# Loading each K and V tile of a decode attention kernel through two DMA queues instead of one

## The chip, the core and the metric

The kernel runs on one core of a Trainium2 chip. The metric is the device time of one execution in microseconds, given as the median over several runs. A core has five engines with instruction streams of their own: PE (matmul), DVE (vector), ACT (scalar activation), POOL (GpSimd) and SP (SyncE, which here only issues transfers). Transfers from the chip's main memory (HBM) to the on-chip buffer are made by 16 DMA engines; SP, ACT and POOL can each put transfers into a queue of its own.

## What is computed

One decode step of attention (8 sequences, 32 heads, 4096 keys, head size 128) and an MLP beside it, on the same normalized input; both are added to x.

```python
xn = _layernorm(x)
q = (xn @ wq).reshape(B, Sq, Hq, Dh).transpose(0, 2, 1, 3)        # B=8, Sq=1, Hq=32, Dh=128
scores = jnp.einsum("bhqd,bhkd->bhqk", q, k_cache) * (Dh ** -0.5)  # Sk=4096 keys
o = jnp.einsum("bhqk,bhkd->bhqd", _softmax(scores), v_cache)
return x + o.reshape(B, Sq, Hq * Dh) @ wo + mlp(layernorm(xn))     # MLP 640 -> 1728 -> 640
```

All inputs are bf16. The two caches are 268 MB each and every byte of them is used once, so nearly everything that is read is cache.

## The kernel before

**Items.** The work is cut into NQ = 32 items: item i is one sequence and a group of HS = 8 heads. The 8 heads of 4096 keys lie over the 128 partitions, 16 partitions for each head and NKEY = 256 keys in each partition. A K tile or a V tile is thus 128 partitions of 256 keys x 128 numbers, 64 KB in a partition and 8.39 MB in all.

**Buffers.** `S_sb` has three slots of one tile each: K of the even items (KA), K of the odd items (KB), and V (VS). K(i) can be loaded when item i-2 is done with its slot, V(i) when item i-1 is done with the only V slot.

**The steps of an item.** `k_ready` is a small POOL memset (`kr_sb`) behind a wait for K(i); PE waits for it. `dve_chunk` (three of them) computes q.k for 176 of the 256 keys on DVE: a multiply by the broadcast query (`qbc_sb`), an add of halves, a reduction into `Sd_sb`. The other 80 keys are transposed on PE (`pe_T`), evicted by ACT (`act_T`) and multiplied on PE (`pe_QK`); `dve_sel` picks their scores. `dve_max` finds the maximum, `act_exp` makes the eight rows of `P_sb`; its end is the ticket `exp`. `pe_PV` multiplies with V in 256 matmuls; its end is the ticket `pv`. `o_norm` on POOL scales the result into `oT_sb`, and `qrep` on POOL prepares the query of the next item once the last `pe_QK` of the present one is done.

**What sets the order.** The order is a table of numbers: `at(pos, fn, i)` records a call, all calls are sorted by `pos`, and each engine gets its instructions in that order. An item is Q = 100 positions long and o = 100 i. K(i) is at o-51, V(i) at o+50, `k_ready` at o-2, `qrep` at o-52, `o_norm` at o+175. SP carries all cache and weight loads in this order; ACT's queue has a few small ones and POOL's none. In SP's stream V(i-1) follows K(i).

**The waits of the loads.** `load_k` waits for `exp` of item i-2 (from item KLATE = 6 on; before that for the last transposes `kt` and the last reduction `km` of item i-2). `load_v` waits for `pv` of item i-1. The next-to-last V tile, V(30), is loaded in two pieces cut at key 192 (`V_CUT`), so that PV can begin on the first. After K(31), V(30), the MLP weights (`load_mlp`, `load_w2b`) and V(31), the last loads are those of wo (`load_wl`, `load_wn`), which take K's second slot when item 31 has let it go. At the end stand PV of item 31, `pe_sel` and `dve_fold`, the last products with wo (`fin_wl`, `fin_wn`) and the store.

Here are the functions that the change touches:

Of the kernel before, what the change touches and what calls it, by code (L numbers as in the profile page):

```python
# [192 lines left out]
def bass_parallel_sum__gqa_block_cached__mixer_channel_mlp__decode_kernel(  # L193
# [19 lines left out]
    NKEY = SK * HS // P  # L213
    NHQ = H // HS
    NQ = NHQ * B
# [15 lines left out]
    KLATE = 6  # L231
    assert NKEY == 256 and NQ == 32
    SLOT = NKEY * DH
    KA, KB, VS = 0, 1, 2
# [2 lines left out]
    NL = 3  # L237
    WN_CUT = (0, 5 * CT, 7 * CT, 7 * CT + CT // 2, HS * CT)
    V_CUT = (0, 192, 256)

    def jp_of(i):
        return 80
# [6 lines left out]
    def kslot(i):  # L249
        return KA if i % 2 == 0 else KB  # L250
# [8 lines left out]
    with ExitStack() as es:  # L259
        sb = lambda name, shape, dt: es.enter_context(nc.sbuf_tensor(name, shape, dt))  # L260
        ps = lambda name, shape, dt: es.enter_context(nc.psum_tensor(name, shape, dt))
        sem = lambda name: es.enter_context(nc.semaphore(name))

        S_sb = sb("S_sb", [P, 3, SLOT], BF)
        tile = [S_sb[:, s, :].rearrange("p (j d) -> p j d", d=DH) for s in range(3)]
# [6 lines left out]
        def scratch(n, rows=P, slot=KB):  # L272
# [71 lines left out]
        pe, dve, act, sp, pool = (_Eng(sem(f"{n}_s")) for n in ("pe", "dve", "act", "sp", "pool"))  # L344
        pe2, act2, fin, fin2 = (_Eng(sem(n)) for n in ("pe2_s", "act2_s", "fin_s", "fin2_s"))
        ld_s = [_Dma(sem(f"ld_s{s}")) for s in range(3)]
        ld_x, ld_b1, ld_b2, ld_wq, ld_w1, ld_w2a, ld_w2b, st_a, st_o = (
            _Dma(sem(n)) for n in ("ld_x", "ld_b1", "ld_b2", "ld_wq", "ld_w1", "ld_w2a", "ld_w2b", "st_a", "st_o"))
        ld_vl = [_Dma(sem(f"ld_vl{q}")) for q in range(1, len(V_CUT) - 1)]
        ld_wl = [_Dma(sem(f"ld_wl{q}")) for q in range(2)]  # L350
        ld_wn = [_Dma(sem(f"ld_wn{q}")) for q in range(len(WN_CUT) - 1)]
        tk = {}
        prog = []

        def at(pos, fn, *a):
            prog.append((pos, len(prog), fn, a))
# [4 lines left out]
        def cache_src(cache, i):  # L361
            hq, b = divmod(i, B)
            return cache[b, hq * HS:(hq + 1) * HS].rearrange("h (p j) d -> (h p) j d", j=NKEY)

        def load_k(i):
            s = kslot(i)
            if i >= KLATE:
                sp.wait(tk[("exp", i - 2)])
            elif i >= 2:
                sp.wait(tk[("kt", i - 2)], tk[("km", i - 2)])  # L370
            elif s == KB:
                sp.wait(tk["qmm"])
            tk[("k", i)] = ld_s[s].sig(sp.dma_start(tile[s], cache_src(A_k_cache, i)))

        def load_mlp():
            sp.wait(tk[("kt", NQ - 2)], tk[("km", NQ - 2)])
# [1 line left out]
            load("w2a", ld_w2a, w2_sb, B_w2[0:FB * P, :].rearrange("(p c) n -> p c n", c=FB))  # L378

        def load_v(i):  # L380
            sp.wait(tk["qmm"] if i == 0 else tk[("pv", i - 1)])
            if i != NQ - 2:
                tk[("v", i)] = [ld_s[VS].sig(sp.dma_start(tile[VS], cache_src(A_v_cache, i)))]
                return
            tk[("v", i)] = []
            for d, lo, hi in zip([ld_s[VS]] + ld_vl, V_CUT[:-1], V_CUT[1:]):
                if lo:
                    d.n += 1
                tk[("v", i)].append(
                    d.sig(sp.dma_start(tile[VS][:, lo:hi, :], cache_src(A_v_cache, i)[:, lo:hi, :])))  # L390

        def load_b1():
            act.wait(tk[("kt", NQ - 2)], tk[("km", NQ - 2)])
# [295 lines left out]
        def pe_PV(i):  # L689
            PVB.use(pe)  # L690
            pe.wait(tk[("exp", i)])
            for j in range(NKEY):
                if j == 0:
                    pe.wait(tk[("v", i)][0])
                elif j in V_CUT:
                    pe.wait_ge(ld_vl[V_CUT.index(j) - 1].sem, 1)
                last = pe.matmul(PV_ps[:, 0:HS], tile[VS][:, j, :], P_sb[:, :, j],
                                 start=(j == 0), stop=(j == NKEY - 1))
            tk[("pv", i)] = PVB.used(pe, pe2.sig(last))
# [112 lines left out]
        at(NQ * Q - 55, load_mlp)  # L812
        at(NQ * Q - 54.9, load_w2b)
        at(-870, load_k, 0)
        at(NQ * Q - 60.1, zero_w2b)
        at(-800, consts_pool)
# [17 lines left out]
        for i in range(NQ):  # L834
            o = i * Q
            last = i == NQ - 1
            if i:
                at(o - 51, load_k, i)
            at(o + 50, load_v, i)
            at(o - 52, qrep, i)  # L840
            at(o - 2, k_ready, i)
            at(o - 11, pe_qbc, i)
            at(o - 10.5, act_qbc, i)
            nt = jp_of(i) // TPB
            w = 42.0 / nt
            for t in range(nt):
                at(o + w * t, pe_T, i, t)
                at(o + w * (t + 0.4), act_T, i, t)
                at(o + w * (t + 1.5), pe_QK, i, t)
            at(o + 2, dve_chunk, i, 0)  # L850
            at(o + 26, dve_chunk, i, 1)
            at(o + 52, dve_sel, i, 0)
            at(o + 55, dve_sel, i, 1)
            at(o + 58, dve_chunk, i, 2)
            at(o + 84, dve_max, i)
            at(o + 90 if i else o + Q + 45, act_exp, i)
            at(o + Q + 48, pe_RS, i)
            at(o + Q + 57, dve_rinv, i)
            at(o + Q + 50, pe_PV, i)
            if not last:  # L860
                at(o + Q + 71, act_O, i)
            at(o + Q + 75, o_norm, i)
# [3 lines left out]
        o = NQ * Q  # L866
# [21 lines left out]
        head, mid, end, cut, done = [], [], [], [], []  # L888
# [55 lines left out]
```

## Time and profile before

| | |
|---|---|
| median of 3 runs | 1281.35 us (1281.34 to 1282.29) |
| profiled execution, first to last instruction (span) | 1280.1 us |
| what lies around the span (median less span) | 1.25 us |
| the profiled execution's own time, span and surroundings | about 1281.35 us |
| bytes moved | 551.99 MB, 431 GB/s over the span |
| busy: DVE, PE, ACT, POOL | 1101.6, 672.0, 477.0, 109.3 us |
| DMA packets | 10785 |

The trace gives each instruction's start and duration, what ended the idle time before it, and for the DMA queues the packets, bytes and the time that the packets took. SPq in a row is an instruction by which SP issues a transfer. A row "A<-B" in the waits says that A's engine sat idle until B was done. All kernel instructions pass through helpers, so their line is L111 or L109; rows are told apart by their tiles.

### The profile page before, as it was taken

What the parts mean: (1) busy time and instruction counts of PE and PEld (TensorE: products, weight loads), DVE (VectorE), ACT (ScalarE), POOL (GpSimd) and SP (SyncE); (2) the same over time, 40 slices, a digit from 0 to 9 for tenths busy, and PEclk for the clock granted to TensorE, in tenths of its full rate; (3) what the DMA queues carried; (4) which work ended last, traced back from release to release, by engine and by line L of the source; (5) the groups of instructions that cost most, each with busy time, mean ns of one, the idle gap of its engine ahead of it and who ended that gap; (6) DMA issues with size and microseconds to landing.
All of it is one profiled execution on the core that took longest, in us unless ns stands there. A gap on an engine that the chain in (4) does not pass through costs nothing.

```text
span 1280.1 us, 34355 instructions
## 1 busy us (share of the span) xinstructions
PE 672.0 (52%) x13906; PEld 573.2 (45%) x13906; DVE 1101.6 (86%) x681; ACT 477.0 (37%) x906; POOL 109.3 (9%) x119
## 2 busy tenths in 40 slices
PE   1636555446645446545456554456454466464476
PEld 1435444335535345444345444345343355353465
DVE  1899999889888889888898888898888898888894
ACT  0524444233444233443234443234442334442331
POOL 0020010000000000000000000000000000000050
PEclk9755565565565556555555555556555656655665
DMA  9999999999999999999999999999999999999998
GB/s 419 427 433 431 432 430 432 442 432 430 430 442 428 432 432 436 436 430 432 432 442 430 430 432 438 432 430 434 436 436 430 432 430 442 432 428 434 432 440 367
DMA packets 10785, 551.99 MB, mean 431 GB/s; under 512 B 1242, under 2 KB 1523, under 8 KB 1812
## 3 DMA queue, kind: packets, MB, share of 16 engines
q1 hardware_dynamic: 10736, 551.79, 99.7%
q8 instruction: 9, 0.15, 0.0%
q10 hardware_dynamic: 36, 0.02, 0.0%
q14 instruction: 4, 0.03, 0.0%
HBM read 551.80 MB, written 0.01 MB: 431 GB/s over the span
## 4 chain that ended last, share of the span: by engine, by line
DMA 47%; DVE 37%; issue 11%; ACT 4%; DVEq 0%; SPq 0%; PE 0%
DMA S_sb<-in_A_k_cache_dram 45%; DVE S_sb L111 26%; DVE Sd_sb L111 8%; ACT P_sb L111 4%; DMA S_sb<-in_A_wo_dram 2%; DVE S_ps L111 1%; DVE mx_sb L111 1%; DVE mbT_sb L111 0%; DVE mxT_sb L111 0%; DVE ri_sb L111 0%; DVE NB_sb L111 0%; DVEq L109 0%; DVE mq_sb L111 0%; DVE mb_sb L111 0%; SPq L111 0%
## 5 line engine op out<-in xcount | busy, mean ns | idle before, releaser
L111 PE MATMUL TR_ps<-ident_bf,S_sb 128*128 128x128 bf16 (+1 forms) x2570 | 343.3, 280 | 353.5 <-POOL kr_sb L111 333.2
L111 DVE TENSOR_TENSOR S_sb<-S_sb,qbc_sb 128x7552 bf16<-128x7552 bf16 (+1 forms) x96 | 388.7, 4049 | 128.3 <-DMA S_sb<-in_A_k_cache_dram 128.0
L111 PEld LDWEIGHTS TR_ps<-ident_bf,S_sb 128*128 (+2 forms) x2570 | 245.7, 103 | 411.7 <-issue 338.5
L111 DVE TENSOR_REDUCE Sd_sb<-S_sb 128x59 f32<-128x3776 bf16 (+1 forms) x96 | 390.2, 4065 | 6.0
L111 ACT ACTIVATE KT_sb<-TR_ps 128x1024 bf16<-128x1024 bf16 x320 | 327.0, 1024 | 121.6 <-PE TR_ps L111 109.6
L111 PE MATMUL PV_ps<-P_sb,S_sb 128*128 128x8 bf16 x8192 | 224.0, 175 | 140.6 <-DMA S_sb<-in_A_v_cache_dram 137.9
L111 PEld LDWEIGHTS PV_ps<-P_sb,S_sb 128*128 128x128 bf16 x8192 | 221.3, 103 | 143.3 <-DMA S_sb<-in_A_v_cache_dram 140.5
L111 DVE TENSOR_TENSOR S_sb<-S_sb 128x3776 bf16<-128x3776 bf16 (+1 forms) x96 | 206.5, 2151 | 3.3
L111 ACT ACTIVATE P_sb<-Sd_sb,NB_sb 128x256 bf16<-128x256 f32 x256 | 126.3, 494 | 210.9 <-DVE NB_sb L111 210.9
L111 PE MATMUL S_ps<-qrep_sb,KT_sb 128*128 128x8 bf16 x2560 | 121.9, 177 | 50.9 <-ACT KT_sb L111 47.8
L111 ACT ACTIVATE oU_sb<-PV_ps 128x8 f32<-128x8 f32 x31 | 5.5, 178 | 375.8 <-PE PV_ps L111 375.8
L111 PEld LDWEIGHTS S_ps<-qrep_sb,KT_sb 128*128 128x128 bf16 x2560 | 91.7, 103 | 82.4 <-ACT KT_sb L111 41.1
L111 POOL TENSOR_TENSOR oT_sb<-oU_sb,ri_sb 128x8 bf16<-128x8 f32 x31 | 71.8, 2315 | 370.8 <-DVE S_sb L111 315.3
L111 POOL COPY qrep_sb<-qT_sb 128x128 bf16<-128x128 bf16 x32 | 18.3, 573 | 474.7 <-PE S_ps L111 455.1
L111 ACT ACTIVATION_READ_ACCUMULATOR P_sb<-Sd_sb,NB_sb 128x1 f32 x256 | 47.8, 187 | 0.0
L111 DVE TENSOR_TENSOR S_ps<-S_ps,mask_sb 128x320 f32<-128x320 f32 (+1 forms) x65 | 31.6, 486 | 2.7 <-PE S_ps L111 2.7
L111 DVE TENSOR_REDUCE Sd_sb<-S_ps 128x40 f32<-128x320 f32 x64 | 31.5, 492 | 2.2
L111 PE MATMUL QB_ps<-ident_bf,qrep_sb 128*128 128x128 bf16 x32 | 9.1, 285 | 40.7 <-DVE S_sb L111 22.1
L111 ACT ACTIVATE qbc_sb<-QB_ps 128x128 bf16<-128x128 f32 x32 | 8.9, 278 | 57.6 <-PE QB_ps L111 57.6
L111 POOL MEMSET kr_sb<- 128x1 f32 x32 | 3.2, 99 | 294.9 <-DMA S_sb<-in_A_k_cache_dram 294.9
L111 PEld LDWEIGHTS QB_ps<-ident_bf,qrep_sb 128*128 128x128 bf16 x32 | 3.3, 103 | 43.6 <-ACT oU_sb L111 29.0
L111 PE MATMUL CH_ps<-rs_sb,ones_f 128*128 128x8 f32 x64 | 15.4, 313 | 6.5 <-ACT P_sb L111 6.5
(68 smaller groups left out, 150.6 us busy)
## 6 DMA issues: line engine op xcount, KB each, us to landing
S_sb<-in_A_v_cache_dram SPq DMA_DIRECT2D x1, 6144.0 KB, 26.8
S_sb<-in_A_wq_dram SPq DMA_DIRECT2D x1, 5120.0 KB, 15.6
S_sb<-in_A_wo_dram SPq DMA_DIRECT2D x1, 2560.0 KB, 18.4
S_sb<-in_B_w_dram SPq DMA_DIRECT2D x1, 2160.0 KB, 30.3
S_sb<-in_B_w_dram SPq DMA_DIRECT2D x1, 2080.0 KB, 34.9
S_sb<-in_A_v_cache_dram SPq DMA_DIRECT2D x1, 2048.0 KB, 31.4
S_sb<-in_A_wo_dram SPq DMA_DIRECT2D x1, 1280.0 KB, 21.1
S_sb<-in_A_wo_dram SPq DMA_DIRECT2D x1, 800.0 KB, 22.6
```

What stands on the lines that cost most here:

```text
L111: inst = getattr(e, name)(*a, **k)
```

## The change

From item 2 on, each K load, and from item 0 on each V load, is written as two loads of 128 keys each: the first half goes into SP's queue as before, the second into POOL's, which thereby issues DMAs for the first time. Each half has its own semaphore (`ld_s` for SP, `ld_g` for POOL) and both have the waits that the whole load had. V(30) becomes three: keys 0 to 96 on SP, 96 to 192 on POOL, 192 to 256 on SP. Who waited for a load now waits for both halves. `load_k` moves from o-51 to o-101 from item 2 on, which places it behind `k_ready` of item i-1 and ahead of `qrep` of item i. K(0), K(1), and all weights are loaded by SP as before.

```diff
+    KH = NKEY // 2
...
+        ld_g = [_Dma(sem(f"ld_g{s}")) for s in range(3)]
...
         def load_k(i):
             s = kslot(i)
-            if i >= KLATE:
-                sp.wait(tk[("exp", i - 2)])
-            elif i >= 2:
-                sp.wait(tk[("kt", i - 2)], tk[("km", i - 2)])
-            elif s == KB:
-                sp.wait(tk["qmm"])
-            tk[("k", i)] = ld_s[s].sig(sp.dma_start(tile[s], cache_src(A_k_cache, i)))
+            if i < 2:
+                if s == KB:
+                    sp.wait(tk["qmm"])
+                tk[("k", i)] = ld_s[s].sig(sp.dma_start(tile[s], cache_src(A_k_cache, i)))
+                return
+            tk[("k", i)] = []
+            for e, d, lo in ((sp, ld_s[s], 0), (pool, ld_g[s], KH)):
+                if i >= KLATE:
+                    e.wait(tk[("exp", i - 2)])
+                else:
+                    e.wait(tk[("kt", i - 2)], tk[("km", i - 2)])
+                tk[("k", i)].append(d.sig(e.dma_start(
+                    tile[s][:, lo:lo + KH, :], cache_src(A_k_cache, i)[:, lo:lo + KH, :])))
...
         def load_v(i):
...
+            end = V_CUT[1] if i == NQ - 2 else NKEY
+            parts = [(sp, ld_s[VS], 0, end // 2), (pool, ld_g[VS], end // 2, end)]
+            if end < NKEY:
+                ld_vl[0].n += 1
+                parts.append((sp, ld_vl[0], end, NKEY))
             tk[("v", i)] = []
+            for e, d, lo, hi in parts:
+                e.wait(tk["qmm"] if i == 0 else tk[("pv", i - 1)])
                 tk[("v", i)].append(
-                    d.sig(sp.dma_start(tile[VS][:, lo:hi, :], cache_src(A_v_cache, i)[:, lo:hi, :])))
+                    d.sig(e.dma_start(tile[VS][:, lo:hi, :], cache_src(A_v_cache, i)[:, lo:hi, :])))
...
-                    pe.wait(tk[("v", i)][0])
+                    pe.wait(tk[("v", i)][:2])
...
-                at(o - 51, load_k, i)
+                at(o - 51 if i < 2 else o - 101, load_k, i)
```

In POOL's stream of the first items, this is what stands there before (`kr_sb` is `k_ready`, `qrep_sb` is `qrep`, `oT_sb` is `o_norm`; rows from `qrep` of item 0 to `o_norm` of item 0, with what each waits for):

```order
L111 COPY qrep_sb<-qT_sb 128x128 [waits dve_s]
L111 MEMSET kr_sb 128x1 [waits ld_s0]
L111 COPY qrep_sb<-qT_sb 128x128 [waits pe_s]
L111 MEMSET oT_sb 128x8
L111 MEMSET kr_sb 128x1 [waits ld_s1]
L111 COPY qrep_sb<-qT_sb 128x128 [waits pe_s]
L111 TENSOR_TENSOR oT_sb<-oU_sb,ri_sb 128x8 [waits dve_s,act_s]
```

And now, from the same `qrep` of item 0 on:

```order
L111 COPY qrep_sb<-qT_sb 128x128 [waits dve_s]
L111 MEMSET kr_sb 128x1 [waits ld_s0]
L111 COPY qrep_sb<-qT_sb 128x128 [waits pe_s]
L111 DMA S_sb<-in_A_v_cache_dram 128x16384
L111 MEMSET oT_sb 128x8
L111 MEMSET kr_sb 128x1 [waits ld_s1]
L111 DMA S_sb<-in_A_k_cache_dram 128x16384 [waits dve_s]
L111 COPY qrep_sb<-qT_sb 128x128 [waits pe_s]
L111 DMA S_sb<-in_A_v_cache_dram 128x16384 [waits pe2_s]
L111 TENSOR_TENSOR oT_sb<-oU_sb,ri_sb 128x8 [waits dve_s,act_s]
```

Behind each `k_ready` there is now the second half of the next K, and between `qrep` and `o_norm` the second half of a V. The first DMA, that of V(0), stands behind `k_ready` of item 0 and `qrep` of item 1, which SP's half does not.

At the end of SP's stream, from K(31) on (a number in a row is the elements in a partition: 16384 is half a tile):

```order
L111 DMA S_sb<-in_A_k_cache_dram 128x16384 [waits act2_s]
L111 DMA S_sb<-in_A_v_cache_dram 128x12288 [waits pe2_s]
L111 DMA S_sb<-in_A_v_cache_dram 128x8192
L111 DMA S_sb<-in_B_w_dram 128x8640 [waits dve_s,pe_s]
L111 DMA S_sb<-in_B_w_dram 128x8320
L111 DMA S_sb<-in_B_w_dram 4x1280 [waits pool_s]
L111 DMA S_sb<-in_B_w_dram 4x1280 x7
L111 DMA S_sb<-in_A_v_cache_dram 128x16384 [waits pe2_s]
```

Before, the rows of K(31) and V(31) had 32768 elements and the first of V(30) had 24576; their places and all rows of the weights (`in_B_w`, `in_A_wo`) are the same. In POOL's stream the second half of V(31) now comes behind the two copies of `sel_pool`:

```order
L111 MEMSET kr_sb 128x1 [waits ld_g1,ld_s1]
L111 MEMSET S_sb 48x1280 [waits dve_s]
L111 COPY S_sb<-ident_bf 128x2048
L111 COPY S_sb<-ident_bf 128x1024
L111 DMA S_sb<-in_A_v_cache_dram 128x16384 [waits pe2_s]
L111 TENSOR_TENSOR oT_sb<-oU_sb,ri_sb 128x8 [waits dve_s,act_s]
```

The DMA row is the only new one; the rest stood in this order before.

More of the change, by code (lines that the diff above doesn't have):

```diff
@@ L380, in load_v @@
         def load_v(i):
[L381 to L384, printed above, removed]
+            end = V_CUT[1] if i == NQ - 2 else NKEY
[3 more added lines that the diff above has]
+                parts.append((sp, ld_vl[0], end, NKEY))
             tk[("v", i)] = []
-            for d, lo, hi in zip([ld_s[VS]] + ld_vl, V_CUT[:-1], V_CUT[1:]):
-                if lo:
-                    d.n += 1
+            for e, d, lo, hi in parts:
+                e.wait(tk["qmm"] if i == 0 else tk[("pv", i - 1)])
                 tk[("v", i)].append(
-                    d.sig(sp.dma_start(tile[VS][:, lo:hi, :], cache_src(A_v_cache, i)[:, lo:hi, :])))
+                    d.sig(e.dma_start(tile[VS][:, lo:hi, :], cache_src(A_v_cache, i)[:, lo:hi, :])))
         def load_b1():
```

## The prediction

> **What bounds the kernel now.** I read the page's slices first, then its DMA queues, then one item of the middle in the timeline.
>
> ```profile
> span 1280.1 us, 34355 instructions
> DMA  9999999999999999999999999999999999999998
> GB/s 419 427 433 431 432 430 432 442 432 430 430 442 428 432 432 436 436 430 432 432 442 430 430 432 438 432 430 434 436 436 430 432 430 442 432 428 434 432 440 367
> q1 hardware_dynamic: 10736, 551.79, 99.7%
> ```
>
> The DMA engines are busy 99.7% of the span with the packets of one queue, SP's, at a flat 430 to 442 GB/s; only the first two slices and the last are lower. So the kernel is bound by how fast the 16 engines move 552 MB. DVE, 86% busy, is second. The next question is how far ahead the loads are issued, since that says what a later issue would cost.
>
> ```profile
> 558.70 0.33 SPq L111 DMA_DIRECT2D S_sb<-in_A_k_cache_dram  x1
> 558.87 4.03 DVE L111 TENSOR_TENSOR S_sb<-S_sb,qbc_sb 128x7424 bf16<-128x7424 bf16 x1 [4.27 <-DMA S_sb<-in_A_k_cache_dram]
> 578.15 7.00 PE L111 MATMUL PV_ps<-P_sb,S_sb 128*128 128x8 bf16 x256 [4.86 <-DMA S_sb<-in_A_v_cache_dram]
> 585.18 0.33 SPq L111 DMA_DIRECT2D S_sb<-in_A_v_cache_dram  x1
> 597.41 0.33 SPq L111 DMA_DIRECT2D S_sb<-in_A_k_cache_dram  x1
> 597.56 4.03 DVE L111 TENSOR_TENSOR S_sb<-S_sb,qbc_sb 128x7424 bf16<-128x7424 bf16 x1 [4.25 <-DMA S_sb<-in_A_k_cache_dram]
> S_sb<-in_A_k_cache_dram SPq DMA_DIRECT2D x32, 38.7
> S_sb<-in_A_v_cache_dram SPq DMA_DIRECT2D x31, 31.6
> ```
>
> An item takes 597.41 - 558.70 = 38.7 us, two loads of 19.35 us. K is issued 38.7 us before it lands: 19.35 us of other loads are still queued ahead of it. V is issued 31.6 us ahead, so 31.6 - 19.35 = 12.3 us are queued. These are the margins: a K half may be issued up to 19 us later, a V half up to 12 us, before the DMA engines run dry. DVE waits 4.27 us per item for K and PE 4.86 us for V; both wait because of the rate, and a load that lands later for a while only uses margin.
>
> **What the change does to the rate.** Bytes stay. What changes is the packets: a half has 128 packets of 32 KB where the whole had 128 of 64 KB, and one more set of 16 semaphore packets. What a packet costs beside its bytes can be read by setting a stretch of 64 KB packets against one of small ones. First the DMA view of 600 to 1200 us, then 1265.7 to 1277 us, when wo is loaded:
>
> ```profile
> DMA packets 4464, 260.05 MB, mean 433 GB/s; under 512 B 496, under 2 KB 496, under 8 KB 496
> q1 hardware_dynamic: 4464, 260.05, 100.1%
> ```
>
> ```profile
> DMA packets 718, 4.55 MB, mean 402 GB/s; under 512 B 76, under 2 KB 237, under 8 KB 493
> q1 hardware_dynamic: 718, 4.55, 96.6%
> ```
>
> Time of packets over all 16 engines: 600 x 16 x 1.001 = 9609.6 us and 11.3 x 16 x 0.966 = 174.7 us. With a us per MB and b us per packet: 260.05a + 4464b = 9609.6 and 4.55a + 718b = 174.7. This gives b = 0.0103 us: 10 ns for each packet.
>
> Added packets per engine: 62 tiles (30 K, 32 V; V(30) goes from two pieces to three, also one more) x (128 / 16 data + 1 semaphore) = 558. Times 10.3 ns: 5.7 us. The first stretch's 100.1% says that neighbouring packets overlap by 0.1%, 1.3 us of the run over 10736 / 16 = 671 packets, 2 ns each; that leaves 8.3 x 558 = 4.6 us. I take **+5 us**.
>
> The trace never has two busy queues side by side, so this term needs both bounds. Below: if the engines serve one queue while the other pays its 10 ns, the added packets cost nothing and those of today vanish too, 671 x 10.3 ns = 6.9 us gained. Above: if going from one queue to the other costs as much again as a packet, 62 x 16 = 992 data packets per engine add 10.2 us, so 5.7 + 10.2 = +15.9. I stay near the single-queue rows: there too the next packet already stands in the queue and 8 ns are paid all the same.
>
> **Issue, waits and order.** SP issues a half in 0.33 us as it did a whole; its order is unchanged. POOL's halves are new. K(i+1)'s stands behind `k_ready` of item i, so it waits for K(i) to land besides `exp`; at 558.70 and 558.79 these coincide:
>
> ```profile
> 558.79 0.10 POOL L111 MEMSET kr_sb<- 128x1 f32 x1 [9.88 <-DMA S_sb<-in_A_k_cache_dram]
> 572.93 0.39 POOL L111 COPY qrep_sb<-qT_sb 128x128 bf16<-128x128 bf16 x1 [14.03 <-PE S_ps L111]
> 585.44 2.19 POOL L111 TENSOR_TENSOR oT_sb<-oU_sb,ri_sb 128x8 bf16<-128x8 f32 x1 [12.12 <-DVE S_sb L111]
> ```
>
> Cost 0, covered by 19 us. V(i)'s half waits for `pv`, which ends just before 585.18; `qrep`, ahead of it, is done by 573.3: cost 0, covered by 12 us. Behind POOL's two waits stand `qrep` (14.03 us after the K half's place) and `o_norm` (idle 12.12 us before): free too. How long POOL is busy issuing one DMA no row shows; the bounds are SP's 0.33 us and its longest compute instructions here, some 5 us each (quoted below). Either fits into 12 us. DVE and PE each wait for one semaphore more, tens of nanoseconds inside 4.27 and 4.86 us of waiting: 0.
>
> At the start POOL's half of V(0) comes behind `qrep` of item 1:
>
> ```profile
> 48.83 1.37 POOL L111 COPY qrep_sb<-qT_sb 128x128 bf16<-128x128 bf16 x1 [12.86 <-PE S_ps L111]
> 55.50 0.10 POOL L111 MEMSET kr_sb<- 128x1 f32 x1 [5.25 <-DMA S_sb<-in_A_k_cache_dram]
> 68.64 0.33 SPq L111 DMA_DIRECT2D S_sb<-in_A_k_cache_dram  x1
> ```
>
> So it is issued at about 50.2 us, beside the last 5.3 us of K(1), which lands by 61 instead of 55.5; DVE is on item 0 until about 68. V's first half is still queued on SP, so no engine idles: 0.
>
> **The end.** It has the least margin.
>
> ```profile
> 1238.33 0.34 SPq L111 DMA_DIRECT2D S_sb<-in_A_v_cache_dram  x1
> 1253.32 2.71 SPq L111 DMA_DIRECT2D S_sb<-in_A_wo_dram  x6
> 1265.62 7.00 PE L111 MATMUL PV_ps<-P_sb,S_sb 128*128 128x8 bf16 x256 [5.92 <-DMA S_sb<-in_A_v_cache_dram]
> 1275.46 1.84 PE L111 MATMUL ACC_ps<-S_sb,oS_sb 128*8 128x160 bf16 x52
> 1277.57 0.65 PE L111 MATMUL ACC_ps<-S_sb,oS_sb 128*8 128x160 bf16 x12 [0.26 <-DMA S_sb<-in_A_wo_dram]
> ```
>
> V(31) lands at 1265.6, the last of wo at 1277.5; PE waits only 0.26 us for the latter. V(31) may thus land 0.3 us later against wo. In the new order POOL's queue is empty when its half of V(31) is issued near 1239, so that half starts at once and shares the engines with the MLP weights; at an even share it needs 2 x 9.7 us and lands near 1259. SP's half follows the weights and lands when all bytes ahead of wo have moved, as before: 0 beside the 5 us. The MLP weights land up to 7 us later; their products were done at 1255, PV waits until 1265: covered.
>
> **Sum.** Profiled execution: 1280.1 us of span + 1.25 around it = 1281.35, equal to the median. 1281.35 + 5 = 1286.35, say **1286.4 us**.
>
> **The rivals.**
>
> *The queues cover each other.* While one queue's packet pays its 10 ns, the other's bytes flow. For it: two queues give an engine two streams to choose from. Against: packets of one queue already stand back to back and still show b. It decides from half of b upward: at half, 0.5 x (671 + 558) x 10.3 = 6.3 us off the 1281.35 + 5.7, 1280.7, no change; in full 1281.35 - 6.9 = 1274.4; I place the case at 1276.
>
> *Nothing measurable.* Part of b is covered, or POOL's packets are cheaper: 1281 to 1283.
>
> *V(31) lands behind wo.* If POOL's queue gets clearly less than half of the engines, its half of V(31) is still under way when SP is on wo. Each us late beyond 0.26 moves the end by one; the most is 1277.5 - 1265.6 = 11.9 us. With b: 1289 to 1298. Against: equal packets on both queues.
>
> *POOL's half is cut smaller than 32 KB.* In n pieces each, it adds (n - 1) x 62 x 8 x 10.3 ns = 5.1 us for each further piece, and POOL's queue gets the smaller share, so the end's price may come on top. n = 2 gives 1291.5, n = 8 1322 and more. No row shows a POOL transfer. [...] In this trace only the hardware queue occurs, with 64 KB packets, so it is untested here.
>
> *DVE holds POOL's issue up.* Rows for such a lock:
>
> ```profile
> 1216.82 1.16 POOL L111 MEMSET S_sb<- 48x1280 bf16 x1
> 1217.92 10.54 POOL L111 COPY S_sb<-ident_bf 128x2048 bf16<-128x2048 bf16 x2
> 1216.84 4.03 DVE L111 TENSOR_TENSOR S_sb<-S_sb,qbc_sb 128x7424 bf16<-128x7424 bf16 x1 [4.27 <-DMA S_sb<-in_A_k_cache_dram]
> 1220.90 5.67 DVE L111 TENSOR_TENSOR S_sb<-S_sb 128x3712 bf16<-128x3712 bf16 x1
> 562.93 2.09 DVE L111 TENSOR_TENSOR S_sb<-S_sb 128x3712 bf16<-128x3712 bf16 x1
> ```
>
> POOL's copies stretched DVE's add from 2.09 to 5.67 us, while POOL's memset, which only writes, ran beside a DVE multiply. If an issue is locked out by the multiply and the add, a K half is 4.03 + 2.09 = 6.1 us late, within 19: nothing. It would have to lose 12 us at every V; each us beyond, in 31 items, is 31 us. At 1 us: 1317. [...]
>
> **How the numbers follow.** My forecast (b is paid in series, +3 to +8) 0.50; nothing measurable 0.17; queues cover each other 0.10; V(31) late 0.09; smaller pieces 0.10; issue held up 0.04. A difference within 0.2% (2.6 us) can't be told from no change. Faster 0.10, same 0.17, slower 0.50 + 0.09 + 0.10 + 0.04 = 0.73. The range 1278.5 to 1298 leaves out most of the covered case, most of smaller pieces and the hold-up, under 2 in 10; it takes in the queue-change bound of +15.9 (1297.3). The forecast's own range is 1284 to 1290.
>
> **What would show it.** Right: a second busy queue of about 260 MB with packets of 32 KB, some 8900 packets more in all, DMA share still over 99%, about 38.85 us from K issue to K issue, waits of DVE and PE for loads as now, and V(31) before wo. Wrong: other packet sizes on the new queue (smaller pieces); slices of the DMA row below 9 (hold-up); a PE wait at the end on V(31) after wo has landed; a rate above 433 GB/s in the middle (cover).

## The result, and the profile after

The changed kernel takes 1286.41 us (median of 5 runs, 1286.24 to 1287.62); the kernel before takes 1281.41 us on the same occasions (5 runs, 1281.34 to 1282.29). The ratio is 1.0040, 95% interval 1.0027 to 1.0052: slower by 5.0 us, or 0.4%. The profiled execution's span is 1285.0 us, 4.9 us longer.

The page of the changed kernel, its span, its slices and its queues (packets, MB, share of 16 engines):

```profile
span 1285.0 us, 34509 instructions
DMA  9999999999999999999999999999999999999998
GB/s 421 414 432 429 432 431 432 430 432 432 428 437 427 436 429 435 429 431 434 430 432 430 434 429 434 430 434 430 431 432 431 431 432 432 430 432 432 429 430 379
q1 hardware_dynamic: 10736, 292.79, 53.0%
q0 software_dynamic: 8928, 259.00, 46.9%
```

The engines are as full as before (99.9% for both queues), the bytes are the same, and there are 8928 packets more. q0, POOL's queue, carried 8928 packets with 259 MB: 992 of them are the semaphores' (62 loads x 16), which leaves 7936 of 32.6 KB on average. So POOL's halves were not cut smaller. The same stretch as in the prediction, 600 to 1200 us, in the DMA view:

```profile
DMA packets 8875, 259.01 MB, mean 432 GB/s; under 512 B 970, under 2 KB 970, under 8 KB 970
q0 software_dynamic: 4436, 129.53, 50.2%
q1 hardware_dynamic: 4438, 129.47, 50.1%
```

In 600 us it moved 259.01 MB where the kernel before moved 260.05: 0.4% less, with twice the packets, and the two queues shared the engines evenly. The trace's record of each single packet shows how: in 99 of 100 cases an engine's next packet is one of the other queue. It starts 3 to 4 ns before the recorded end of the one ahead of it, just as with one queue in the kernel before. One item in the timeline:

```profile
561.57 0.33 SPq L111 DMA_DIRECT2D S_sb<-in_A_k_cache_dram  x1
561.84 0.10 POOL L111 MEMSET kr_sb<- 128x1 f32 x1 [10.05 <-DMA S_sb<-in_A_k_cache_dram]
562.00 4.03 DVE L111 TENSOR_TENSOR S_sb<-S_sb,qbc_sb 128x7424 bf16<-128x7424 bf16 x1 [4.53 <-DMA S_sb<-in_A_k_cache_dram]
562.08 0.57 POOL L111 DMA_DIRECT2D S_sb<-in_A_k_cache_dram  x1
588.28 0.33 SPq L111 DMA_DIRECT2D S_sb<-in_A_v_cache_dram  x1
588.55 0.53 POOL L111 DMA_DIRECT2D S_sb<-in_A_v_cache_dram  x1 [12.11 <-DVE S_sb L111]
1144.49 0.33 SPq L111 DMA_DIRECT2D S_sb<-in_A_k_cache_dram  x1
```

From the K issue at 561.57 to that at 1144.49 there are 15 items: 38.86 us each, against 38.70 before. POOL issues its half 0.3 to 0.5 us behind SP and is busy with it for 0.53 to 0.57 us, also while DVE runs the multiply. Waits still end with the loads: DVE's for K grew from 4.27 to 4.53 us. The end:

```profile
1261.55 2.27 PE L111 MATMUL ACC_ps<-S_sb 128*8 128x160 bf16 x60 [3.12 <-DMA S_sb<-in_B_w_dram]
1270.57 7.00 PE L111 MATMUL PV_ps<-P_sb,S_sb 128*128 128x8 bf16 x256 [5.40 <-DMA S_sb<-in_A_v_cache_dram]
1281.72 0.52 PE L111 MATMUL ACC_ps<-S_sb,oS_sb 128*8 128x160 bf16 x20 [0.24 <-DMA S_sb<-in_A_wo_dram]
1282.52 0.65 PE L111 MATMUL ACC_ps<-S_sb,oS_sb 128*8 128x160 bf16 x12 [0.28 <-DMA S_sb<-in_A_wo_dram]
```

V(31) lands ahead of wo, 4.95 us later than before. PE waits 0.24 and 0.28 us for wo where it waited 0.26 us once, but the last products start 11.95 us after PV's start in both kernels (1282.52 - 1270.57, before 1277.57 - 1265.62). The MLP's products wait 3.12 us for their weights, which share the engines with V(31)'s second half now; PV's wait covers that.

### The profile page after: what moved, and what is told of

It is laid out like the page before. It is cut to its first block, busy times and chain, and to the rows that moved or that the text cites. A ratio compares the mean times of both kernels' runs of the same rounds, so it can differ in the third digit from the quotient of the medians.

```text
span 1285.0 us, 34509 instructions
## 1 busy us (share of the span) xinstructions
PE 670.8 (52%) x13906; PEld 572.2 (45%) x13906; DVE 1101.6 (86%) x681; ACT 476.8 (37%) x906; POOL 127.8 (10%) x181
## 3 DMA queue, kind: packets, MB, share of 16 engines
q0 software_dynamic: 8928, 259.00, 46.9%
## 4 chain that ended last, share of the span: by engine, by line
DMA 47%; DVE 37%; issue 11%; ACT 4%; SPq 0%; DVEq 0%; PE 0%
DMA S_sb<-in_A_k_cache_dram 45%; DVE S_sb L111 26%; DVE Sd_sb L111 7%; ACT P_sb L111 4%; DMA S_sb<-in_A_wo_dram 2%; DVE S_ps L111 1%; DVE mx_sb L111 1%; DVE mxT_sb L111 0%; DVE mbT_sb L111 0%; SPq L111 0%; DVE ri_sb L111 0%; DVEq L109 0%; DVE NB_sb L111 0%; DVE mq_sb L111 0%; DVE mb_sb L111 0%
## 5 line engine op out<-in xcount | busy, mean ns | idle before, releaser
L111 POOL TENSOR_TENSOR oT_sb<-oU_sb,ri_sb 128x8 bf16<-128x8 f32 x31 | 55.9, 1804 | 10.3 <-DVE ri_sb L111 5.7
L111 POOL DMA_DIRECT2D S_sb<-in_A_v_cache_dram x32 | 17.1, 535 | 362.4 <-DVE S_sb L111 316.3
```

The lines of the kernel that those rows point to most:

```text
L111: inst = getattr(e, name)(*a, **k)
```

## The experiments

Theory P is the prediction's: each packet costs some 8 to 10 ns on its engine, in whichever queue. Theory Q: the cost is that of a second queue or of POOL's part in it. The kernel before was run beside each group; its medians there were 1281.52, 1281.39 and 1281.45 us.

**Halves in one queue** (`e1_halves_sp`). The kernel before with

```diff
+    PIECES = 2
...
+            n = PIECES if i >= 2 else 1
+            for c in range(n):
+                lo, hi = c * NKEY // n, (c + 1) * NKEY // n
+                tk[("k", i)] = ld_s[s].sig(sp.dma_start(
+                    tile[s][:, lo:hi, :], cache_src(A_k_cache, i)[:, lo:hi, :]))
```

and the same for V (of V(30), its first 192 keys).

> Both halves of each tile in SP's queue, one behind the other; POOL issues no DMA. The packets are those of the changed kernel (558 more per engine than before), the second queue is gone. Theory P (a packet costs 8 to 10 ns on its engine in whichever queue, and nothing else matters): 4.6 to 5.7 us over before, 1286 to 1287, and 38.85 us from one K issue to the next. Theory Q (the cost is that of serving a second queue, or of POOL's issue): no change, 1281.4, and 38.70 us per item.

Measured: 1286.05 us (1285.85 to 1286.46), ratio 1.0034 (1.0021 to 1.0047). The DMA view of 600 to 1200 us and two K issues:

```profile
DMA packets 8890, 259.17 MB, mean 432 GB/s; under 512 B 980, under 2 KB 980, under 8 KB 980
q1 hardware_dynamic: 8889, 259.17, 100.4%
560.53 0.80 SPq L111 DMA_DIRECT2D S_sb<-in_A_k_cache_dram  x2
1143.38 0.80 SPq L111 DMA_DIRECT2D S_sb<-in_A_k_cache_dram  x2
```

38.86 us per item, as with two queues: 4.5 of the 5.0 us are there with one queue, which decides for P against Q. 4.53 us over 558 packets are 8.1 ns each.

**Quarters in one queue** (`e2_quarters_sp`): `PIECES = 4`.

> Four pieces of 16 KB per partition in SP's queue (V(30): its first 192 keys in four). Added packets per engine: 62 x 3 x 9 = 1674. Theory P: 13.9 us at 8.3 ns, 17.2 at 10.3 ns: 1295 to 1299, 39.15 us per item. If the cost were one per piece issued and not per packet it would still be three times that of the halves; if only the semaphore packets cost, the same ratio, so this run gives the size and not the kind. Theory Q: 1281.4.

Measured: 1295.33 us (1295.27 to 1295.65), ratio 1.0107 (1.0092 to 1.0122).

```profile
DMA packets 17657, 257.11 MB, mean 429 GB/s; under 512 B 1964, under 2 KB 1964, under 8 KB 1964
q1 hardware_dynamic: 17656, 257.11, 100.7%
```

13.81 us over 1674 packets: 8.2 ns. The cost grows with the number of pieces, at one price.

Data packets, semaphore packets and loads grow in step in these two runs, so the times alone do not say which of them pays. The packet records do. On average a 64 KB packet took 2.422 us, a 32 KB packet 1.217 us (half of 2.422 is 1.211), a 16 KB packet 0.615 us and a semaphore packet 0.009 us. A split thus adds 12 ns for a further data packet and 9 ns for a further semaphore packet. Less the 3 to 4 ns by which neighbours overlap, the 496 data and 62 semaphore packets that the halves add on each engine make some 4.7 us, over nine tenths of it from the data packets.

**One queue, POOL's** (`e5_pool`). Whole loads, nearly all issued by POOL:

```diff
+            e = pool if i >= 2 else sp
...
-            tk[("k", i)] = ld_s[s].sig(sp.dma_start(tile[s], cache_src(A_k_cache, i)))
+            tk[("k", i)] = (ld_g if i >= 2 else ld_s)[s].sig(e.dma_start(tile[s], cache_src(A_k_cache, i)))
```

with all V, the MLP weights and wo changed likewise.

> One queue again, but POOL's: all K loads from the third on, all V loads, the MLP weights and wo as whole loads issued by POOL (SP keeps wq, K(0), K(1) and the last 64 keys of V(30)). Packets as before. Theory P: no change within 1 us, 1281 to 1282.5. Theory Q in the form that POOL's queue is the dearer one: over 1284, with more than 38.70 us per item.

Measured: 1283.49 us (1282.97 to 1283.63), ratio 1.0013 (1.0005 to 1.0022): 1 us more than P allowed. The middle, 600 to 1200 us:

```profile
DMA packets 4464, 259.99 MB, mean 433 GB/s; under 512 B 496, under 2 KB 496, under 8 KB 496
q0 software_dynamic: 4463, 259.98, 100.1%
```

That is nearly the middle of the kernel before (260.05 MB), so POOL's queue is not dearer by packet or byte. The difference lies at the ends, some 0.9 us in the first four items and 1 us after item 30, where loads stand behind other POOL work; which of it costs was not tried.

**Partition halves on two queues, and on one** (`e3_parts`, `e12_parts_sp`). To have two queues with 64 KB packets, SP takes partitions 0 to 63 and POOL 64 to 127:

```diff
-            for e, d, lo in ((sp, ld_s[s], 0), (pool, ld_g[s], KH)):
+            for e, d, lo in ((sp, ld_s[s], 0), (pool, ld_g[s], P // 2)):
...
-                    tile[s][:, lo:lo + KH, :], cache_src(A_k_cache, i)[:, lo:lo + KH, :])))
+                    tile[s][lo:lo + P // 2], cache_src(A_k_cache, i)[lo:lo + P // 2])))
```

> Two queues as in the changed kernel, but SP loads partitions 0 to 63 and POOL 64 to 127 of all keys, so that packets stay at 64 KB and only one semaphore packet per tile and engine is added (62). Theory P: 0.5 us over before, about 1282. Theory Q: as the changed kernel, 1286 or more. A third outcome, if half the partitions can't take the full rate: a lower rate in the middle and well over 1290, which would tell neither.

Measured: 2436.29 us (2333.59 to 2471.11; the profiled run took 2471.11), the third outcome. Its middle:

```profile
DMA packets 2493, 131.79 MB, mean 220 GB/s; under 512 B 482, under 2 KB 482, under 8 KB 482
q1 hardware_dynamic: 1247, 65.86, 50.3%
q0 software_dynamic: 1246, 65.93, 50.2%
```

The engines are as busy as before (50.3 + 50.2%), at half the rate: a 64 KB packet took 4.79 us on average where it took 2.42. Then both halves in SP's queue:

> Each tile as two loads of 64 partitions, both in SP's queue, partitions 0 to 63 ahead of 64 to 127; packets of 64 KB, one queue. It tells what made the kernel with partition halves on two queues take 2436 us with packets of twice the usual duration. If it is the half of the partitions in one load: again about 2400 us, 218 GB/s in the middle. If it was the two queues side by side: about 1282 us, one semaphore packet more per tile.

Measured: 2580.71 us in its one run (before beside it: 1282.06), and

```profile
DMA packets 2371, 124.86 MB, mean 208 GB/s; under 512 B 465, under 2 KB 465, under 8 KB 465
q1 hardware_dynamic: 2370, 124.85, 100.1%
```

So the half rate comes with loads of 64 partitions and needs no second queue; two loads for each tile alone, as in `e1_halves_sp`, cost only 4.5 us. These two say nothing on P and Q.

**K in one queue, V in the other** (`e6_k_pool_v_sp`). Whole loads; `load_k` as in `e5_pool`, all else on SP.

> Two queues with whole 64 KB packets: K from the third on in POOL's queue, all V and the weights in SP's. As many packets as before. A K and a V load now run side by side, at half rate each while both are in flight: if V's queue idles during the 7 us of PV and K's likewise 7 us before its next issue, both need about 31.7 us from issue to landing (24.7 shared, 7 alone) and the item stays at 38.70 us. Theory P: 1281 to 1283 and 38.70 us per item. Theory Q (going from queue to queue costs something per packet): the middle slower than 38.70, at 10 ns per packet 38.86 us per item and 1286 or more.

Measured: 1362.32 us (1357.34 to 1372.0), ratio 1.0637 (1.0604 to 1.0669). Neither theory had that.

```profile
q1 hardware_dynamic: 2096, 122.68, 48.7%
q0 software_dynamic: 2096, 122.68, 47.2%
S_sb<-in_A_v_cache_dram SPq DMA_DIRECT2D x14, 34.0
S_sb<-in_A_k_cache_dram POOLq DMA_DIRECT2D x14, 35.6
```

The engines stand idle for 4% of the middle (48.7 + 47.2). A V load that shares the engines with K lands 34.0 us after its issue; with 7.0 us of PV before the next issue that is 41 us, more than the 38.7 of the item. So the round from one V load through PV to the next V load became the bound. With the 31.7 us of my even split it would just have fitted; why it took 34.0 us was not tried. That going from queue to queue is free is carried by halves in one queue against the changed kernel (1286.05 and 1286.41 us), not by this run.

**Late issues** (`e7_delay_in_margin`, `e8_delay_past_margin`, `e10_delay_half`). The prediction let a V half be issued 12 us late. Here memsets of a spare tile stand ahead of POOL's V half, each waiting for the one before:

```diff
+                if e is pool and 0 < i < NQ - 2:
+                    for _ in range(HOLD):
+                        t = hold.sig(pool.memset(hold_sb[:, :], 0.0))
+                        pool.wait(t)
```

HOLD is 16, 40 and 8 in the order of the names.

> The changed kernel with 16 memsets of a spare tile on POOL, one behind the other, between the wait and the issue of each second half of V(1) to V(29): the half is issued some 8 us later. Nothing else is changed. Theory C (the 12 us queued ahead of V cover a late issue): within 1 us of the changed kernel, 1286 to 1287.5, with POOL's V half landing a few us later. Theory D (a late POOL half is felt at once because SP's half can't be used alone): up to 8 us in each of 29 items, 1290 to 1500.

> The same with 40 memsets, some 20 us, past the 12 us. POOL's own queue is then empty for about 8 us per item, in which the engines have only SP's half (9.7 us) to work on; the V half lands 20 + 19.4 = 39.4 us after the wait at an even share, at best 29.7 if it has the engines alone, and PV adds 7 before the next. Theory C: slower only now, 0 to 8 us in each of 29 items: 1290 to 1500, with the V wait of PE several times as long. If it stays at 1287 the margin is larger than I read it.

> The changed kernel with POOL's V halves alone issued 8 memsets, some 4.2 us, after the wait. Theory F (the queues being two, POOL's half issued late is overtaken by SP's half and by SP's half of the next K, which is issued 12 us after the V wait): little, since 4 us later it still finds POOL's half of K ahead of it: 1286 to 1290. Theory G: about half of what 8.4 us did (20.5 us over the changed kernel): some 1297.

Measured: HOLD 8 (4.2 us) 1287.63 us (1287.47 to 1288.11); HOLD 16 (8.4 us) 1306.91 us (1305.56 to 1308.63); HOLD 40 1433.55 us in its one run. With HOLD 8 the middle is that of the changed kernel:

```profile
590.75 4.18 POOL L111 MEMSET hold_sb<- 128x448 f32 x8 [12.03 <-PE PV_ps L111]
602.82 0.33 SPq L111 DMA_DIRECT2D S_sb<-in_A_k_cache_dram  x1
1030.28 0.33 SPq L111 DMA_DIRECT2D S_sb<-in_A_k_cache_dram  x1
```

11 items of 38.86 us, so in the middle 4.2 us are covered. What it lost, it lost early: it is 2.3 us behind the changed kernel when K(8) is issued (291.98 us against 289.69) and still 2.3 us when K(30) is (1146.79 against 1144.49), and about 1 us of that is won back at the end. Theory F had this right (1286 to 1290), G's 1297 did not come.

At 8.4 us, inside my 12, an item costs about 0.7 us more ((1306.91 - 1286.41) / 29). Theory C fell. D's wide range holds the time, but not D's reason: by it the 4.2 us would have been felt in every item too. The 0.7 us need not be the price of a late V half alone, though: the memsets also hold up what stands behind them in POOL's stream: `k_ready`, and POOL's half of the next K, issued at 615.06 us where SP's is issued at 609.40.

With HOLD 40 this side effect is all that is left:

```profile
620.92 4.03 DVE L111 TENSOR_TENSOR S_sb<-S_sb,qbc_sb 128x7424 bf16<-128x7424 bf16 x1 [0.34 <-issue]
637.39 0.09 POOL L111 MEMSET kr_sb<- 128x1 f32 x1
637.79 2.31 PE L111 MATMUL TR_ps<-ident_bf,S_sb 128*128 128x128 bf16 x16 [21.95 <-POOL kr_sb L111]
651.42 6.97 PE L111 MATMUL PV_ps<-P_sb,S_sb 128*128 128x8 bf16 x256
```

DVE starts on K at 620.92, but `k_ready` comes 16.5 us later and PE sits idle for 21.95 us until then; PV, which should have waited several times as long for V, waits for nothing. This run says nothing on the margin.

**The same lateness without the halves** (`e9_one_queue_delay`, `e11_both_late`). The kernel before with each whole V load 8.4 us late, and the changed kernel with both V halves late:

```diff
+            if 0 < i < NQ - 2:
+                pool.wait(tk[("pv", i - 1)])
+                for _ in range(HOLD):
+                    t = hold.sig(pool.memset(hold_sb[:, :], 0.0))
+                    pool.wait(t)
+                sp.wait(t)
```

> The kernel before, with whole loads in SP's queue, where each V load from V(1) to V(29) is issued some 8.4 us after its wait (behind the 16 memsets on POOL). Theory F (a load that is issued late in a first-come queue lands when it would have, as long as bytes are queued ahead of it, 12 us here): 1281 to 1283. Theory G (that margin does not exist: landing plus the 7 us of PV already fill an item, 31.6 + 7.0 of 38.7): the delay goes on top of every item, 1300 or more, up to 29 x 8.4 = 244 us.

> The changed kernel with both V halves issued some 8.4 us after the wait, so that neither is ahead of the other. Theory F: the loss of the uneven issue (1307) goes away, 1286 to 1289. Theory G: no better than with POOL's half alone late, 1307 or more. A value between tells that the memsets' other effect, POOL's half of the next K held up behind them, takes part.

Measured: 1309.61 us (1308.88 to 1310.78) and 1327.07 us (1326.52 to 1327.54). Theory F fell in both: the loss needs no second queue and no uneven issue. In the middle of the one-queue run `k_ready` is not held up: POOL still waits 3.73 us for K before the `k_ready` at 613.24. G is half right: the times are over 1300 and over 1307, but not every us goes on top (28 us, not 244). The margin is smaller than I read it. A part of the reason shows in packets of under 512 B, each the end of one engine's share of a load. In the kernel before, K's 16 fall between 594.9 and 597.1 us, two of them in the first 0.7 us; with whole V loads late, between 609.5 and 613, two in the first 0.3 us:

```profile
DMA packets 32, 1.05 MB, mean 477 GB/s; under 512 B 16, under 2 KB 16, under 8 KB 16
DMA packets 4, 0.13 MB, mean 187 GB/s; under 512 B 2, under 2 KB 2, under 8 KB 2
```

```profile
609.22 0.33 SPq L111 DMA_DIRECT2D S_sb<-in_A_v_cache_dram  x1
DMA packets 33, 1.11 MB, mean 318 GB/s; under 512 B 16, under 2 KB 16, under 8 KB 16
DMA packets 2, 0.00 MB, mean 0 GB/s; under 512 B 2, under 2 KB 2, under 8 KB 2
```

A load lands when the last of 16 engines is done: the last of K's 16 packets starts at 597.00 in the kernel before, and POOL and DVE, which wait for K, start at 597.50 and 597.56. The first is done about 2 us earlier in the kernel before and about 3 us here, and can go on only if the next load is already there. Before, V is issued at 585.18 and the first engine runs out after 594.9: 9.7 us, not 12.3. Late by 8.4 us it is issued at 609.22, at most 0.6 us ahead of that, and from 609.5 to 613 us packets start at 318 GB/s. Nor did this load start when it was issued: from 608.9 to 610.18 us only semaphore packets start, so the first data of this V came 1 us behind its issue.

```profile
DMA packets 10, 0.00 MB, mean 0 GB/s; under 512 B 10, under 2 KB 10, under 8 KB 10
```

That leaves some 8.7 us, with nothing to spare against 8.4. How the loss then comes about is known only in part. The stretch of 600 to 1200 us with whole V loads late:

```profile
DMA packets 4369, 254.64 MB, mean 424 GB/s; under 512 B 480, under 2 KB 480, under 8 KB 480
q1 hardware_dynamic: 4365, 254.61, 99.5%
```

Against the 260.05 MB and 100.1% of the kernel before, 2.1% of the bytes are missing, some 0.8 us per item, but only 0.6% of the busy time, some 0.2 us. So engines that stand idle are the smaller part. The larger part is packets that take longer: 332 of the 3885 packets of 64 KB took over 2.5 us here, up to 4.2, and they lie around the start of the late V loads; before, none took over 2.44. Why they take longer was not tried, and why both halves late cost more than whole loads late is not explained either.

## Why the prediction was right

**The term of packets**, +4.6 to +5.7 us with +5 taken, is shown: 4.53 us with the same packets in one queue, 13.81 us with three times as many added, 8.1 and 8.2 ns each, and by the packet records nearly all of it lies in the data packets. The prediction's 8.3 ns was a difference of two parts that were each too small: 10.3 ns for any packet, where the records have 12 for a data packet and 9 for a semaphore's, less an overlap of 2 ns, where they have 3 to 4. So the mechanism was right, and the size owes something to luck. That the total is right to 0.1 us is chance: 5.0 us were measured, and the 0.4 us between two queues and one (1286.41 and 1286.05) are less than the intervals can tell apart.

**Both bounds of that term** were too wide. The queues don't cover each other's packets (the shares are 50.2 + 50.1 = 100.3% with two queues and 100.4% with one), and going from queue to queue, which the engines do at nearly every packet, adds nothing that shows.

**Issue, waits and order at 0** held: POOL's issue takes 0.53 to 0.57 us and comes 0.3 to 0.5 us behind SP's, far inside any margin. DVE does not hold it up: POOL issued its K half at 562.08, in 0.57 us, inside the 4.03 us multiply from 562.00, and its V half at 588.55, in 0.53 us, inside DVE's 2.12 us add from 588.54. The added semaphores show as 15 further records of a semaphore wait on DVE and 32 on PE, of 21 and 51 ns each.

**The margin of 12 us was wrong.** The step is "31.6 - 19.35 = 12.3 us are queued ... a V half up to 12 us": it takes a landing for the moment when all engines run out, and an issue for the moment when the data start. In the middle, POOL's V halves bore 4.2 us at no cost, and whole V loads in one queue did not bear 8.4 us; the 19 us that the same step gives for K were not tried. The change used 0.27 + 0.53 = 0.8 us of it, so the error cost the forecast nothing. By the same step "each us beyond, in 31 items, is 31 us" is no price either: one queue lost 28 us where the whole delay was 8.4 us per item.

**The start at 0** was nearly so: K(1) landed 1.2 us later than before and K(2) 1.4 us, but the K issues behind them, at 68.63, 102.86 and 137.46 us, came within 0.1 us of those before. **The end at 0** held: V(31) and the last products both moved by 4.95 us. POOL's half of V(31) did not start at once, though: issued at 1243.74, it has its first packet at 1247.40 and lands 22.4 us after its issue, at about 1266, not 1259; PV's start at 1270.57 covers that. One reading of the rate was off, with nothing resting on it: two slices of the middle stand at 428 GB/s, below the 430 to 442 that the prediction names. **Smaller pieces** did not come about: POOL's data packets are of 32.6 KB on average, so that no run shows the further pieces behind 1291.5 and 1322 us. The smaller share that goes with smaller packets does show, from 1250 to 1258 us, where 71 packets of V(31) in q0 (2.33 MB, 32.8 KB each) took 67.4% of the engines' time and 77 packets in q1 (1.06 MB, 13.8 KB) 30.9%.

No run was faster than the kernel before: its packets are whole rows of 64 KB, and each split by keys adds to their number.

## What to carry to other kernels

Here, with the transfer engines full (99.7% of the span), another queue brought nothing (halves took 1286.41 us in two queues, 1286.05 in one), and splitting the loads cost what the added packets cost (8.1 to 8.2 ns each). Where the engines are full, look for the price of a packet in two stretches of the same trace with different packet sizes, and multiply. A margin read as "issue to landing less the load's own time" is too long by the time between the first and the last engine's end of a load (here 2 to 3 us) and by the time from an issue to its first data (here 1 us, and 3.7 us for POOL's half of V(31)), so try it with a delay before building on it, and check that the delay holds up nothing else. And a load that is split between queues should be split so that each part still covers all 128 partitions: here halves of 64 partitions ran at 220 GB/s, halves of the keys at 432.

## What was not expected of the hardware

Loads of 64 partitions ran at 208 GB/s in one queue and 220 in two, against 433 with 128 partitions and the same 64 KB packets, with the engines 100% busy all the while. In two queues a 64 KB packet took 4.79 us on average instead of 2.42. The 220 GB/s show that two such transfers side by side, one for each half of the partitions, do not make up for it. What makes the packets slow no run shows.
